# Two attention stretches per block of a squared-ReLU layer: from steps 1 and 8 to steps 3 and 10

## The chip, the cores and the metric

The kernel runs on one core of a Trainium2 chip. The metric is the device time of one execution in microseconds (us); the median of several runs is compared. TensorE (PE) does the matmuls, VectorE (DVE) and ScalarE (ACT) the element-wise work, GpSimd (POOL) gathers and scatters, and SyncE (SP) issues nearly all DMA transfers in one queue.

## The reference, cut to what matters

Three layers follow each other on 3072 tokens (4 sequences of 768) of width 384 (8 heads of 48).

```python
# 1. attention with a decaying state
state = alpha[:, :, t, :, None] * state + k_t v_t^T      # for each t
y[:, :, t] = q_t @ state
# 2. squared ReLU, 384 -> 2048 -> 384
h = x @ w_in; g = max(h, 0) ** 2; x = g @ w_out
# 3. eight experts, each token goes to one: 384 -> 1024 -> 384
e = argmax(x @ w_gate + modality_bias[modality_id])
out[e] = gate_w * (max(x[e] @ w1[e], 0) @ w2[e])
```

## The kernel before, in words

Attention is cut into 24 units `u` of 128 tokens, all heads of one sequence at a time; two sequences take turns, six units each. For one unit DVE first scans the decays (`a_scan`, `a_scan2`, lines 314 to 333: two scans, two products that scale k and q in place). Then PE does a stretch of small matmuls: `finish(u - 1)` (line 832) computes the output `py` of the unit before (lines 389 and 392) and its state update `kv` (line 374), and `a_p(u)` and `a_kt(u)` compute the scores `pp` (line 342) and a transpose `pk` (line 356). `group(u)` (line 838) is this whole stretch. ACT copies `py` to `y` (line 394), which SP writes to a DRAM scratch `yt_d` (line 397); `finish` also issues the loads of unit `u + 1`.

The squared-ReLU layer works in 12 blocks `n` of 256 tokens (two units). A block has 16 steps, one for each 128 of the 2048 inner columns. At a step PE does layer 1 (`layer1`, nine matmuls of 256 columns into `ph`, three for each of three 128-row parts, since every fp32 factor is split in a high and a low part), and then layer 2 of the step three before (`moe1_l2`, line 864, six matmuls of 392 columns into the two accumulators `po`). ACT and DVE make `g` out of `ph` (lines 985 and 992) and split it (`gh` line 996, `gl` line 998). `ph` has two buffers. `po` is two banks, and there are only two banks for it, so the first layer-2 matmul of a block (at its step 3, three steps after its first layer-1 matmul) can start only when the result of the block before has been read out of both: `lg` (line 873, DVE), then `ob` (line 874 on ACT, line 875 on DVE). That block's last layer-2 matmul is at step 2 of the present block. The input of a block comes from `yt_d`: `a_yload` (line 401, tile `xf`) reads it, and `a_x` splits it into `xh` (line 407, ACT) and `xl` (line 408, DVE), at the latest for the block's step 0.

Blocks 0 and 1 are interleaved with LEAD = 8 in the first 32 steps; the diff doesn't touch their list but for the scans of unit 7. From block 2 on every block has the two stretches of `GA` (line 772), of units 2n+3 and 2n+4, and the scans of a unit stand 4 and 2 steps ahead of its stretch. Blocks 2 to 10 hold units 7 to 23 and the last `finish`; block 11 has none. Steps are collected with `put` (line 886) and run ahead of the layer-1 matmuls of their step. Other entries of the list are the routing to experts (`ROUTE`, line 770, at steps 3, 5 and 9 to 14: `lg` to one-hot, then on PE `pr` at step 9 and `ptab` at step 13, in the PSUM bank "ms" that `kv` and `pk` also use) and the check of the decays (line 424).

The order by hand is that of PE alone: `with tc.manual_schedule(engines={mybir.EngineType.PE})` (line 974). ACT, DVE, POOL and SP get an order when the program is built, in which the place in the list is only one thing that counts, and readiness another; on the chip each then works its own queue in that order.

Of the kernel before, what the change touches and what calls it, by code (L numbers as in the profile page):

```python
# [179 lines left out]
def gla_moe_moe2(ctx: ExitStack, tc: tile.TileContext, ain, vin, al_d, wio_d, wg_d, wgt_d, mid_d, mb_d, w12_d, out):  # L180
# [133 lines left out]
    def a_scan(u):  # L314
        al, qk, v = attn_in.pop(u)
        q, k = qk[:, 0:HP * C], qk[:, HP * C:]
        ar3 = p2.tile([HR, HP, C + 1], F32, name="ar")
        ar = ar3.rearrange("p g t -> p (g t)")
        mul = dve if u < MULD else pool
        dve.tensor_tensor_scan(out=ar, data0=al[:, 0:HP * (C + 1)], data1=delta.rearrange("p g t -> p (g t)"), initial=0.0, op0=ALU.mult, op1=ALU.add)  # L320
        mul.tensor_tensor(out=k.rearrange("p (g t) -> p g t", g=HP), in0=k.rearrange("p (g t) -> p g t", g=HP), in1=ar3[:, :, 0:C], op=ALU.mult)
        ac = ar3[:, :, C:C + 1]

        inv = d1[:, 1:].rearrange("p (g t) -> p g t", g=HP)[:, :, C:]
        dve.tensor_scalar(out=inv, in0=ac, scalar1=PROD_MIN, scalar2=None, op0=ALU.max)
        dve.reciprocal(out=inv, in_=inv)
        un[u] = dict(q=q, k=k, v=v, ac=ac, al=al, mul=mul)

    def a_scan2(u):
        q, al, mul = (un[u][i] for i in ("q", "al", "mul"))  # L330
        af = p1.tile([HR, HP * (C + 1) + 1], F32, name="af")
        dve.tensor_tensor_scan(out=af, data0=al[:, ::-1], data1=d1[:, ::-1], initial=0.0, op0=ALU.mult, op1=ALU.add)
        mul.tensor_tensor(out=q.rearrange("p (g t) -> p g t", g=HP), in0=q.rearrange("p (g t) -> p g t", g=HP), in1=af[:, 1:].rearrange("p (g t) -> p g t", g=HP)[:, :, 0:C], op=ALU.mult)
# [3 lines left out]
    def a_p(u):  # L337
        x = un[u]
        pp = [ps1.tile([128, HP, C], F32, tag=t, name="pp") if u in ATG else ps2.tile([128, HP, C], F32, tag="out" if u == 1 else "P", name="pp") for t in ("ms", "y")]
        for hp in range(HP):  # L340
            for j, (r0, r1) in enumerate(((0, 64), (64, HR))):
                pe.matmul(out=pp[j][:, hp, :], lhsT=x["k"][r0:r1, hp * C:(hp + 1) * C], rhs=x["q"][r0:r1, (HP - 1 - hp) * C:(HP - hp) * C], start=True, stop=True)
        x["pt"] = []
        for j in range(2):
            if u in (1, 3):
                pt = p3.tile([128, 2, XW], F32, tag="ob", name="pt").rearrange("p j d -> p (j d)")[:, 0:HP * C].rearrange("p (g t) -> p g t", g=HP)
            else:
                pt = p1.tile([128, HP, C], F32, tag=f"pt{j}", name="pt")
            dve.tensor_tensor(out=pt.bitcast(I32), in0=pp[j].bitcast(I32), in1=mask[:, None, :].to_broadcast([128, HP, C]), op=ALU.bitwise_and)
            x["pt"].append(pt)  # L350

    def a_kt(u):
        x = un[u]
        pk = ps1.tile([128, HP, HR], F32, tag="ms", name="pk")
        for hp in range(HP):
            pe.transpose(out=pk[:, hp, :], in_=x["k"][:, hp * C:(hp + 1) * C], identity=ident[0:HR, 0:HR])
        kt = p1.tile([128, HP, HR], F32, name="kt")
        act.copy(out=kt, in_=pk)
        x["kt"] = kt

    def a_scale(u):
        if u // 2 % CPB:
            t = st_t[u % 2][:, :, 0:D]
            dve.tensor_tensor(out=t, in0=t, in1=un[u]["ac"].to_broadcast([HR, HP, D]), op=ALU.mult)
# [34 lines left out]
    def a_yload(n):  # L399
        x = p1.tile([128, ND, TB], F32, name="xf")  # L400
        sp.dma_start(out=x, in_=yt_d.rearrange("(d p) t -> p d t", p=128)[:, :, n * TB:(n + 1) * TB])
        xt[n] = x

    def a_x(n):
        xh = p2.tile([128, ND, TB], F32R, name="xh")
        xl = p2.tile([128, ND, TB], F32R, name="xl")
        act.copy(out=xh, in_=xt[n])  # L407
        dve.tensor_tensor(out=xl, in0=xt[n], in1=xh, op=ALU.subtract)  # L408
        xt[n] = (xh, xl)
# [359 lines left out]
    ROUTE0 = 14, 15, 16, 17, 18, 19, 20, 21  # L769
    ROUTE = 3, 5, 9, 10, 11, 12, 13, 14  # L770
    ROUTEZ = 3, 3, 4, 5, 6, 6, 7, 8
    GA = 1, 8
    PRE = 4
    LEAD = 8
    LAG1 = 3
# [7 lines left out]
    if True:  # L783
# [48 lines left out]
        def finish(u, load=True):  # L832
            a_y(u)
            a_state(u)
            if load and u + 2 < NU:
                load_attn(u + 2)

        def group(u):

            finish(u - 1)  # L840
            if u < NU:
                a_p(u)
                a_kt(u)
                a_scale(u)
# [41 lines left out]
        def put(gs, *steps):  # L886
            at.setdefault(gs, []).extend(steps)
# [44 lines left out]
        for n in range(2, NB):  # L932
            g0 = two + (n - 2) * NF
            for i in range(2):
                u = 2 * n + 3 + i
                if u <= NU:
                    put(g0 + GA[i] + 2 * (u == 7), lambda u=u: group(u))
                    if u < NU:
                        put(g0 + GA[i] - 4, lambda u=u: a_scan(u))
                        put(g0 + GA[i] - 2, lambda u=u: a_scan2(u))  # L940
            if n < NB - 1:
                put(g0 + 12, lambda n=n: a_yload(n + 1))
                put(g0 + 15, lambda n=n: a_x(n + 1))
        g0 = two + (NB - 3) * NF
# [10 lines left out]
        for m in range(NB - 1):  # L955
# [7 lines left out]
            g0 = two + (m - 1) * NF  # L963
            spread([g0 + k for k in (ROUTE if 0 < m < NB - 2 else ROUTE0 if m == 0 else ROUTEZ)], route())
        for i in range(NA):
            g0 = two + (3 + i // 2) * NF + 8 * (i % 2)
# [157 lines left out]
```

## Time and profile before

| | |
|---|---|
| median of 3 runs | 825.29 us (824.69 to 828.78) |
| profiled execution | 822.23 us, its span 820.4 us |
| PE, PE weight loads | busy 769.2 us (94%), 738.6 us (90%) |
| DVE, ACT, POOL | busy 543.6 us (66%), 402.6 us (49%), 64.5 us (8%) |
| DMA | 105.39 MB, mean 128 GB/s |
| mean granted TensorE clock | 0.974 |

The page gives busy time of each engine, then the span in 40 slices of 20.5 us with the busy share in tenths. Blocks 2 to 10 lie at about 148 to 538 us. Times in the rows are counted from the start of the span. A wait is the time an engine stood idle ahead of an instruction, with the instruction that released it.

### The profile page before, as it was taken

Reading aid. Unit: us, or ns where it says so; the run is one execution under the profiler, and the core shown is the slowest. Engines: PE = TensorE matmul, PEld = TensorE weight load, DVE = VectorE, ACT = ScalarE, POOL = GpSimd, SP = SyncE. Lnnn points to the kernel's source line nnn. Section 1 sums busy time; section 2 is a strip of 40 time slices with the busy share of each in tenths; the row PEclk is TensorE's granted clock in tenths of the full one; section 3 lists DMA queues with packets and bytes.
Section 4 is the critical chain, followed back from the end, with each engine's and each line's share of the span. In section 5 each row is a group of like instructions: output and inputs, shape, how many; then the busy total and the mean of one; then the engine's idle time right before and its main releaser. Section 6 shows DMA issues by size and latency. Waiting matters only on the chain. (4 is left out here: it accounts for less than half of the span.)

```text
span 820.4 us, 16492 instructions
## 1 busy us (share of the span) xinstructions
PE 769.2 (94%) x6174; PEld 738.6 (90%) x6174; DVE 543.6 (66%) x1370; ACT 402.6 (49%) x895; POOL 64.5 (8%) x85
## 2 busy tenths in 40 slices
PE   6589999999999999999999999999899999999992
PEld 4478989999998998999999999999889999999992
DVE  8889985776665664676767554456896666666631
ACT  2467879533333333333333333334666666666631
POOL 1000000000000000000000000002013322223110
PEclk9599999999999999999999999999999999999996
DMA  8877566232313211222222211105878777777600
GB/s 241 232 198 219 173 182 192 63 87 56 90 50 103 62 58 39 81 61 76 63 64 64 64 30 30 30 20 172 248 241 240 237 218 230 227 224 231 194 30 18
DMA packets 56019, 105.39 MB, mean 128 GB/s; under 512 B 9163, under 2 KB 29141, under 8 KB 55920
## 3 DMA queue, kind: packets, MB, share of 16 engines
q1 hardware_dynamic: 52720, 94.49, 39.2%
q0 software_dynamic: 3200, 9.65, 3.4%
q8 instruction: 53, 0.87, 0.5%
q14 instruction: 46, 0.38, 0.2%
HBM read 89.95 MB, written 14.36 MB: 127 GB/s over the span
## 5 line engine op out<-in xcount | busy, mean ns | idle before, releaser
L430 PE MATMUL ph<-xh,wh 128*128 128x256 f32 x864 | 249.7, 289 | 7.9 <-ACT xh L407 4.8
L430 PE MATMUL ph<-xl,wh 128*128 128x256 f32 x864 | 243.0, 281 | 1.5 <-DVE xl L408 1.5
L430 PE MATMUL ph<-xh,wl 128*128 128x256 f32 x864 | 243.0, 281 | 0.0
L430 PE MATMUL po<-wh,gh 128*128 128x392 f32 (+1 forms) x584 | 201.6, 345 | 9.4 <-ACT ob L874 5.7
L430 PE MATMUL po<-wh,gl 128*128 128x392 f32 (+1 forms) x584 | 198.3, 340 | 0.0
L430 PE MATMUL po<-wl,gh 128*128 128x392 f32 (+1 forms) x584 | 198.2, 339 | 0.0
L430 PEld LDWEIGHTS ph<-xh,wh 128*128 128x128 f32 x864 | 163.5, 189 | 10.9 <-ACT xh L407 5.1
L430 PEld LDWEIGHTS ph<-xl,wh 128*128 128x128 f32 x864 | 163.8, 190 | 1.8 <-DVE xl L408 1.8
L430 PEld LDWEIGHTS ph<-xh,wl 128*128 128x128 f32 x864 | 163.5, 189 | 0.0
L260 DVE TENSOR_TENSOR wl<-st,wh 128x768 fp32r<-128x768 f32 x104 | 99.5, 957 | 62.5 <-ACT wh L259 62.5
L996 ACT CAST gh<-g 128x256 fp32r<-128x256 f32 x192 | 77.9, 406 | 116.5 <-DVE g L992 116.1
L998 DVE TENSOR_TENSOR gl<-g,gh 128x256 fp32r<-128x256 f32 x192 | 80.8, 421 | 62.3 <-ACT gh L996 61.9
L430 PEld LDWEIGHTS po<-wh,gh 128*128 128x128 f32 x584 | 110.1, 189 | 11.5 <-ACT ob L874 6.9
L985 ACT ACTIVATE g<-ph 128x256 f32<-128x256 f32 x192 | 73.6, 383 | 94.9 <-PE ph L430 94.6
L259 ACT CAST wh<-st 128x768 fp32r<-128x768 f32 x104 | 86.7, 834 | 56.0 <-PE po L430 42.6
L992 DVE SCALAR_TENSOR_TENSOR g<-ph,g 128x256 f32<-128x256 f32 x160 | 67.3, 421 | 66.1 <-ACT g L985 65.7
L430 PEld LDWEIGHTS po<-wl,gh 128*128 128x128 f32 x584 | 110.3, 189 | 0.0
L430 PEld LDWEIGHTS po<-wh,gl 128*128 128x128 f32 x584 | 110.0, 188 | 0.2 <-DVE gl L998 0.2
L727 ACT ACTIVATE gh<-ph 128x256 fp32r<-128x256 f32 x96 | 37.0, 386 | 22.3 <-PE ph L430 20.3
L729 DVE SCALAR_TENSOR_TENSOR gl<-ph,gh 128x256 fp32r<-128x256 f32 x96 | 40.0, 417 | 8.6 <-ACT gh L727 8.5
L563 POOL IOTA row<- 1x96 f32 x1 | 0.2, 234 | 473.7 <-PE py L389 473.7
L745 POOL DMA_INDIRECT out_dram<-xs,ix x25 | 27.3, 1093 | 114.9 <-ACT xs L744 59.6
(187 smaller groups left out, 817.0 us busy)
## 6 DMA issues: line engine op xcount, KB each, us to landing
st<-in_w_dram SPq DMA_DIRECT2D x104, 384.0 KB, 3.9
st<-in_wio_dram SPq DMA_DIRECT2D x32, 384.0 KB, 4.0
qk<-in_ain_dram SPq DMA_DIRECT2D x23, 448.0 KB, 4.2
al<-in_ain_dram SPq DMA_DIRECT2D x24, 226.2 KB, 2.9
v<-in_vin_dram SPq DMA_DIRECT2D x24, 224.0 KB, 3.3
scr<-ob SPq DMA_DIRECT2D x12, 385.0 KB, 3.0
yt_d<-y SPq DMA_DIRECT2D x48, 96.0 KB, 2.8
xf<-yt_d SPq DMA_DIRECT2D x12, 384.0 KB, 3.5
```

Of the source, the lines that this page charges most:

```text
L259: act.copy(out=hi[:, 0:2 * DM], in_=t)
L260: lo_eng.tensor_tensor(out=lo[:, 0:2 * DM], in0=t, in1=hi[:, 0:2 * DM], op=ALU.subtract)
L430: pe.matmul(out=out_, lhsT=lhs[a][lsl], rhs=rhs[b][rsl], start=first and i == 0, stop=last and i == 2)
L563: pool.iota(thr, pattern=[[0, E], [SLOT, NJ]], base=0, channel_multiplier=0, allow_small_or_imprecise_dtypes=True)
L727: act.activation(out=gh[:, cols], in_=h, func=AF.Relu)
L729: dve.scalar_tensor_tensor(out=gl[:, cols], in0=h, scalar=0.0, in1=gh[:, cols], op0=ALU.max, op1=ALU.subtract)
L745: pool.indirect_dma_start(out=out[:, :], out_offset=bass.IndirectOffsetOnAxis(ap=x["ix"][:, 2 + j:3 + j], axis=0), in_=xo[:, 0:DM], in_off ...
L985: act.activation(out=g, in_=ph, func=AF.Relu)
L992: dve.scalar_tensor_tensor(out=g, in0=ph, scalar=0.0, in1=g, op0=ALU.max, op1=ALU.mult)
L996: act.copy(out=gh, in_=g)
L998: (pool if n in POOLGL else dve).tensor_tensor(out=gl, in0=g, in1=gh, op=ALU.subtract)
```

## The change

The two numbers of `GA` become 3 and 10, and the special case that put unit 7 two steps later falls away (unit 7 stands at step 3 either way). So eight stretches (units 9, 11, ... 23) move from step 1 to step 3 of blocks 3 to 10, nine (8, 10, ... 22 and the last `finish`) from step 8 to step 10 of blocks 2 to 10, and the scans of units 7 to 23 move by two steps in the list.

```diff
-    GA = 1, 8
+    GA = 3, 10
...
                 if u <= NU:
-                    put(g0 + GA[i] + 2 * (u == 7), lambda u=u: group(u))
+                    put(g0 + GA[i], lambda u=u: group(u))
                     if u < NU:
                         put(g0 + GA[i] - 4, lambda u=u: a_scan(u))
                         put(g0 + GA[i] - 2, lambda u=u: a_scan2(u))
```

## Rows read from the trace of the kernel before

**Rows 1.** The page: busy time of the engines, and the granted TensorE clock.

```profile
PE 769.2 (94%) x6174; PEld 738.6 (90%) x6174; DVE 543.6 (66%) x1370; ACT 402.6 (49%) x895; POOL 64.5 (8%) x85
...
PEclk9599999999999999999999999999999999999996
```

**Rows 2.** Waits of PE in blocks 2 to 10: us, times, longest.

```profile
PE po L430 <- ACT ob L874: 5.7, 6, 1.2
PE ph L430 <- DVE g L992: 2.2, 2, 1.9
```

**Rows 3.** Windows: step 3 of blocks 3 and 4, and the sum for blocks 3 to 8.

```profile
core 0: us, PE busy (x) PEld busy (x) DVE busy (x) ACT busy (x) POOL busy (x), PEclk, DMA share, GB/s
201.52:204.81 3.29, 2.40 (x16) 2.19 (x16) 3.22 (x15) 1.51 (x5) 0.00 (x0) 1.00 0.27 70
245.21:248.84 3.63, 2.41 (x17) 2.20 (x17) 3.63 (x17) 1.53 (x5) 0.00 (x0) 1.00 0.26 64
...
sum 20.12, PE 14.41 PEld 13.20 DVE 19.84 ACT 8.97 POOL 0.00; mean PE 2.40 PEld 2.20 DVE 3.31 ACT 1.50 POOL 0.00
```

**Rows 4.** Windows: step 3 of blocks 2, 9; block 8's steps 0 (with stretch), 4; block 5's 11.

```profile
158.48:160.90 2.42, 2.42 (x20) 2.42 (x19) 2.38 (x5) 0.92 (x2) 0.00 (x0) 1.00 0.88 249
465.19:467.49 2.30, 2.30 (x16) 2.19 (x16) 2.19 (x12) 1.36 (x5) 0.00 (x0) 1.00 0.00 0
410.79:416.95 6.16, 6.16 (x85) 5.56 (x84) 2.59 (x7) 1.78 (x4) 0.00 (x0) 1.00 0.26 75
424.60:426.73 2.13, 2.13 (x16) 2.13 (x16) 1.27 (x8) 0.56 (x2) 0.00 (x0) 1.00 0.39 144
309.94:314.17 4.23, 2.31 (x16) 1.98 (x15) 2.12 (x5) 1.21 (x4) 0.00 (x0) 1.00 0.03 9
```

**Rows 5.** Timeline, DVE, ACT and PE in steps 2 and 3 of block 8.

```profile
420.67 1.24 DVE L332 TENSOR_TENSOR_SCAN af<-al,d 112x517 f32<-112x517 f32 x1
...
422.48 0.23 DVE L873 TENSOR_TENSOR lg<-po,bias 128x8 f32<-128x8 f32 x2
...
422.90 0.47 ACT L874 COPY ob<-po 128x384 f32<-128x384 f32 x1
...
423.43 0.45 PE L430 MATMUL po<-wh,gh 128*128 128x392 f32 x1 [0.89 <-ACT ob L874]
```

**Rows 6.** Timeline, PE, DVE and ACT around the stretch of step 3 of block 2.

```profile
154.53 1.08 PE L389 MATMUL py<-qk,state 64*64 64x128 f32 x16
...
159.64 0.34 PE L430 MATMUL po<-wh,gh 128*128 128x392 f32 x1
...
154.38 0.42 DVE L873 TENSOR_TENSOR lg<-po,bias 128x8 f32<-128x8 f32 x2
...
154.81 0.47 ACT L874 COPY ob<-po 128x384 f32<-128x384 f32 x1
```

**Rows 7.** Timeline, DVE after the stretch at step 8 of block 8.

```profile
435.80 0.35 DVE L377 TENSOR_TENSOR state<-state,kv 112x192 f32<-112x192 f32 x1 [1.76 <-PE kv L374]
...
445.21 0.95 DVE L408 TENSOR_TENSOR xl<-xf,xh 128x768 fp32r<-128x768 f32 x1
...
447.30 0.43 DVE L998 TENSOR_TENSOR gl<-g,gh 128x256 fp32r<-128x256 f32 x1 [0.47 <-ACT gh L996]
```

**Rows 8.** Timeline, PE: first layer-1 matmul of block 9.

```profile
454.68 0.28 PE L430 MATMUL ph<-xh,wh 128*128 128x256 f32 x1
```

**Rows 9.** Timeline, DVE and PE: `xl` of block 5, and its first layer-1 matmul.

```profile
270.89 0.95 DVE L408 TENSOR_TENSOR xl<-xf,xh 128x768 fp32r<-128x768 f32 x1
...
278.99 0.28 PE L430 MATMUL ph<-xh,wh 128*128 128x256 f32 x1
```

**Rows 10.** Timeline, SP and ACT: the read of `xf` for block 6, and what waits.

```profile
306.77 0.33 SPq L230 DMA_DIRECT2D al<-in_ain_dram  x1
307.20 0.38 SPq L401 DMA_DIRECT2D xf<-yt_d  x1
...
311.96 0.83 ACT L407 CAST xh<-xf 128x768 fp32r<-128x768 f32 x1 [1.94 <-DMA xf<-yt_d]
312.70 0.38 ACT L985 ACTIVATE g<-ph 128x256 f32<-128x256 f32 x1
```

**Rows 11.** Waits of all engines over the span: ACT's for `xf`.

```profile
ACT xh L407 <- DMA xf<-yt_d: 5.7, 4, 2.1
```

**Rows 12.** Timeline, ACT: one of the decay checks of line 424.

```profile
109.93 0.93 ACT L424 ACTIVATE x<-st,abias 128x768 bf16<-128x768 f32 x1
```

## The prediction

> **What bounds the kernel now.** I read the page first: PE is busy 94% of the span and its weight loads 90%, DVE 66%, ACT 49% [rows 1]. So only what makes PE wait is worth anything, and the total of its matmuls doesn't change here. Next the waits of PE in the stretch that the change touches, blocks 2 to 10. There are only two kinds [rows 2]: six waits of a layer-2 matmul for the copy of `ob`, 5.7 us together, and two waits of a layer-1 matmul for a late `g`, 2.2 us. Then the windows, step by step. A plain step takes 2.13 us [rows 4]. Step 3 of blocks 3 to 8 takes 3.29 to 3.63 us, 20.12 us for the six [rows 3]; in block 9 it takes 2.30 us [rows 4]. Last the timeline of one of them [rows 5]: a scan of 1.24 us starts on DVE at 420.67, so `lg` starts only at 422.48, ACT's `ob` runs from 422.90 to 423.37, and PE, whose layer 1 of that step is done, starts `po` at 423.43. All of this is the exchange of the two `po` banks: the old result has to be out of both before the new block's first layer-2 matmul, and between the two stands one layer 1 of about 1.05 us (nine matmuls, step 3 up to 422.4). The granted clock is 1.00 in every window [rows 3, 4], so no term of mine comes from the clock.
>
> **The change, part by part.**
>
> *The stretch from step 1 to step 3, eight times.* A step with a stretch takes 6.16 us against 2.13 [rows 4], so a stretch costs PE 4.03 us wherever it stands. At step 3 it lies between the last layer-2 matmul of the old block (step 2) and the first of the new (step 3): the read-out of `po` gets 4.03 + 1.05 = 5.1 us in place of 1.05. What it needs now is 1.05 + about 1.1 = 2.2 us, so it is covered with almost 3 us to spare. Block 2 shows this arrangement already, since its stretch stands at step 3 [rows 6]: `lg` starts at 154.38, `ob` on ACT ends at 155.28, the stretch starts at 154.53, and the new `po` starts only at 159.64. Block 2 is not full proof, as its accumulators don't share the banks of the block before; but the read-out is done 4.4 us ahead of where it would be waited for. Gain: 20.12 - 6 x 2.13 = 7.3 us in blocks 3 to 8, and 2.30 - 2.13 = 0.2 us in block 9: 7.5 us.
>
> What the profile calls idle is less, 5.7 us [rows 2]. The page's own legend says that ends of matmuls are modelled; the window has no such end in it, and the first `po` matmul is drawn as 0.45 us long [rows 5]. The Trainium skill (Perfetto Trace Analysis, section Tensor Engine Instruction (MATMUL, LD_WEIGHTS)) says that a matmul's end is computed from its size and not observed. By that rule the start-to-start windows count, and the trace agrees; by the idle alone the gain would be 5.7 us, which I keep as the lower bound.
>
> *The stretch from step 8 to step 10, nine times.* Nothing waits around step 8 or 10. The distances between stretches stay: 7 steps and 9 steps, before and after. So `pt`, `kt`, the state, the loads of the next units and the slots they wait for keep their places against each other, and the `y` writes and loads on SP keep their order. SP is moved past one thing, the write of `ob` by the routing, one DMA per block, which nothing in the block waits for. POOL is passed by none of it (0.00, x0, in these windows [rows 3, 4]).
>
> What shrinks is the distance to the block's end, by two steps, 4.26 us: `y` is written, read back as `xf` and split into `xh` and `xl` for the next block's step 0. In block 8 `xl` ends at 446.16 [rows 7] and block 9 starts at 454.68 [rows 8], 8.5 us later; the tightest is block 5, with 271.84 against 278.99 [rows 9], 7.15 us. After the change 4.3 and 2.9 us are left. I cost this at nothing; what hides it is layers 1 and 2 of the last steps, and if that cover went, every us of lateness would be paid once per block, nine times.
>
> The other neighbour is the routing's `pr` at step 9, whose bank `kv` needs at step 10. DVE is the one to free it, by one small add. Ahead of `kv` PE has a step and the `py` matmuls, over 4 us, and at step 9 DVE no longer has the load that follows a stretch. Cost nothing; bound, one scan ahead of the add, 1.24 us [rows 5], of which 4 us of cover take all.
>
> *DVE after a stretch.* After the stretch at step 8 DVE is busy without a break from 435.80 until its next wait before 447.30 [rows 7], while PE in block 8 loses nothing there. At step 3 the read-out of `ob` and the small operations of the routing come on top, but they start when the stretch does, at a time when PE produces no `ph`. In block 2, with just these neighbours, step 3 takes 2.42 us [rows 4] from its layer 1 to the next, with more matmuls in it (x20) than a plain step (x16): the end of the stretch, and a `ptab`, which stands at step 4 there. So I cost it at nothing.
>
> *Unit 7's scans* stand two steps later in the list, though its stretch doesn't move. DVE's order isn't that of the list: the decay checks of the list's block 5 and later run at 109.93 [rows 12]. The bound is one scan, 1.24 us [rows 5], either way.
>
> *Sum.* 7.5 us, less 0.5 us that I take off for small new waits on a reordered DVE queue (an estimate: less than half of that one scan). The profiled execution of 822.2 us becomes 815.2 us. The median of the runs stands 3.1 us above it, at 825.3 us; the gain is the same, so 818.3 us.
>
> **The rivals.**
>
> *More late g's, small.* The late `g` is real: block 5's step 11 takes 4.23 us instead of 2.13 [rows 4]. The way it comes about [rows 10]: SP issues `al` at 306.77, when the scan that still read its slot has ended, and behind it, at 307.20, the read of `xf`. ACT's queue has `xh` next and waits 1.94 us for `xf`; the `g` behind it starts at 312.70, and PE has both `ph` buffers full. If the new order does this in two more blocks, 2 x 2.1 = 4.2 us of the 7.0 go: 822.5 us, no difference that can be told. For it: ACT waited for `xf` four times [rows 11]. Against it: only two of these reached PE [rows 2], and the change moves the whole chain as one.
>
> *The same, in every block: slower.* One mechanism, the read of `xf` behind another DMA in SP's queue, with `xh` at the head of ACT's. The break-even is 7.0 / 2.1 = 3.3 further blocks; from six on it is slower by over 0.5%. If the seven of nine blocks that don't show it now pay 2.1 us each, that is 14.7 - 7.0 = 7.7 us more than before: 833 us. The Trainium skill (Perfetto Trace Analysis, the same section) says that ACT and DVE work strictly in the order of their queues, so a waiting `xh` holds up a `g` that is ready; the trace agrees, by those 1.94 us. Against it: the waits of ACT for `xf` are 5.7 us over the whole span [rows 11], and the loads keep their distance from the stretch.
>
> *The exchange of `po` isn't relieved.* If the new queues put `lg` or ACT's `ob` behind the stretch's own work (`y`, `state`, the masks), the wait stays: 825.3 us. For it: the order of ACT and DVE is made anew when the program is built. Against it: `py`'s copy can't be ready before some 2 us of the stretch, and block 2 has `ob` first [rows 6].
>
> **How the numbers follow.** A measurement of this kernel can tell about 0.5%, 4.1 us, from no change. The forecast gets 0.76: six waits of one kind, with their length, and a cover more than twice as long. The small rival gets 0.12, the unrelieved exchange 0.05; together 0.17 within 0.5%. The slow one gets 0.07. The forecast's own range is 9.9 us of gain (7.5, and the late `g`'s in blocks 5 and 4 gone too, 2.1 and some 0.3) to 5.7 us: 815.4 to 819.6. To hold 8 in 10 I take in the small rival with 1.5 us for the spread of the medians: 815.4 to 824.0.
>
> **What would show it.** Right: no wait of `po` for `ob` in blocks 3 to 8, except perhaps in block 11; step 3 with its stretch 6.2 us up to its layer 1 and 2.2 us after; steps 1 and 8 plain. The time from a block's start to the next 43.9 us before in block 8, 42.7 us after. `xl` ends 3 to 4 us ahead of its block. Wrong: the same number of waits of `po`, a wait of a layer-1 matmul for `xh` or `xl` at a block's step 0, or late `g`'s at steps 12 to 14 in more than three blocks.

## The result, and the profile after

The changed kernel takes 814.59 us (median of 6 runs, 813.84 to 815.88), the kernel before 824.99 us beside it (6 runs): a ratio of 0.9869, 95% interval 0.9844 to 0.9894 (8.7 to 12.9 us). It is faster, as forecast, but by more than forecast: 814.59 us lies 0.8 us below the lower end of the range. The profiled execution takes 814.26 us, its span 812.5 us.

The page of the kernel after, the lines that answer to [rows 1]: PE does the same work in a shorter span, and one more slice with a lower granted clock (8 tenths) appears late in it.

```profile
PE 768.0 (95%) x6174; PEld 738.4 (91%) x6174; DVE 548.7 (68%) x1370; ACT 403.2 (50%) x895; POOL 68.0 (8%) x85
...
PEclk9599999999999999999999999999899999999997
```

The waits of PE in blocks 2 to 10 of the kernel after, beside [rows 2] (us, times, longest): the six waits of `po` for `ob` are gone, and the two late `g`'s (a layer-1 matmul that waits for a `g` to free its `ph` buffer) are down from 2.2 us to 0.9. Nothing else makes PE wait there.

```profile
PE ph L430 <- DVE g L992: 0.9, 2, 0.5
```

The window of step 3 of block 3 of the kernel after, and the sum for blocks 3 to 8, beside [rows 3] (its columns): 13.36 us in place of 20.12. Step 3 is now the step after a stretch, and takes 2.22 to 2.23 us where a plain one takes 2.13 [rows 4].

```profile
201.45:203.67 2.22, 2.22 (x18) 2.22 (x17) 2.19 (x5) 0.92 (x2) 0.00 (x0) 1.00 0.84 264
...
sum 13.36, PE 13.36 PEld 13.36 DVE 12.84 ACT 5.51 POOL 0.00; mean PE 2.23 PEld 2.23 DVE 2.14 ACT 0.92 POOL 0.00
```

Where the time went, by windows of whole blocks. First the kernel before: block 5, block 8, blocks 2 to 10 together, and all that comes behind them.

```profile
278.99:323.03 44.04, 41.22 (x350) 39.66 (x349) 28.08 (x79) 15.72 (x39) 0.00 (x0) 1.00 0.21 59
410.79:454.68 43.89, 43.00 (x381) 41.43 (x381) 28.75 (x81) 15.69 (x39) 0.00 (x0) 1.00 0.20 60
...
147.93:537.95 390.02, 382.14 (x3309) 367.53 (x3309) 246.12 (x708) 143.42 (x356) 0.52 (x2) 1.00 0.22 62
537.95:820.40 282.45, 262.62 (x1857) 259.06 (x1856) 175.45 (x394) 160.85 (x303) 61.07 (x63) 0.97 0.60 184
```

Then the same four of the kernel after.

```profile
276.24:317.61 41.37, 40.91 (x350) 39.55 (x349) 27.71 (x79) 15.62 (x39) 0.00 (x0) 1.00 0.23 63
403.25:445.96 42.71, 42.71 (x381) 41.34 (x381) 29.60 (x81) 15.73 (x39) 0.00 (x0) 1.00 0.22 61
...
147.96:529.01 381.05, 380.11 (x3309) 366.84 (x3309) 250.97 (x708) 143.86 (x356) 0.62 (x2) 1.00 0.23 63
529.01:812.50 283.49, 263.78 (x1857) 260.44 (x1856) 175.62 (x394) 160.86 (x303) 64.45 (x63) 0.97 0.61 183
```

Blocks 2 to 10 are 8.97 us shorter. A block whose only difference is the exchange of `po`, block 8, gives 1.18 us; block 5 gives 2.67 us, 1.49 us more, because its late `g` of step 11 [rows 4] is gone (a smaller one stands at step 13 now). Behind block 10 the kernel after is 1.04 us longer in this profile; the granted clock there differs from profile to profile (last section).

### The profile page after: what moved, and what is told of

Its sections match the earlier page's. It is cut to its first block, busy times and chain, and to the rows that moved or that the text cites. A ratio compares the mean times of both kernels' runs of the same rounds, so it can differ in the third digit from the quotient of the medians.

```text
span 812.5 us, 16487 instructions
## 1 busy us (share of the span) xinstructions
PE 768.0 (95%) x6174; PEld 738.4 (91%) x6174; DVE 548.7 (68%) x1370; ACT 403.2 (50%) x895; POOL 68.0 (8%) x85
## 5 line engine op out<-in xcount | busy, mean ns | idle before, releaser
L683 POOL DMA_INDIRECT xs<-scr,ix x25 | 32.5, 1301 | 69.7 <-PE px L414 24.6
```

The costliest lines, as they stand in the source:

```text
L683: pool.indirect_dma_start(out=xs[:, j, 0:XW], out_offset=None, in_=scr[0:rows, :], in_offset=bass.IndirectOffsetOnAxis(ap=ix[:, j:j + 1], ...
```

## The experiments

### Which of the two stretches

The first stretch alone is moved:

```diff
-    GA = 1, 8
+    GA = 3, 8
-                    put(g0 + GA[i] + 2 * (u == 7), lambda u=u: group(u))
+                    put(g0 + GA[i], lambda u=u: group(u))
```

> Stretches at 3 and 8: the first one is moved, the second stays. Cover (the stretch stands between the last layer-2 matmul of the old block and the first of the new): the six waits of po for ob are gone, 7.3 us of step time in blocks 3 to 8, so 6.5 to 8 us faster than before. Backlog (DVE no longer has the work after a stretch in front of lg): the same. If the second stretch carries part of the gain: the late g of block 5 (2.1 us) and block 4 (0.4 us) stays here, and this kernel lies about 1.5 us above the changed one.

Or the second alone:

```diff
-    GA = 1, 8
+    GA = 1, 10
```

> Stretches at 1 and 10: only the second one is moved. Cover and backlog: six waits of po for ob stay, 5.7 us of idle, step 3 of blocks 3 to 8 stays at 3.3 us; the time is that of before less at most 1.5 us for a shorter late g. If the second stretch carries the gain: 4 us or more faster than before.

The first alone gives 815.24 us (ratio 0.9884, 0.9855 to 0.9913), the second alone 821.38 us (0.9974, 0.9952 to 0.9995). So the first stretch carries nearly all of it. With the second alone the waits of PE in blocks 2 to 10 are those of before. The late `g`'s take 1.7 us in place of 2.2, but two further profiles of the kernel before have 1.7 and 1.8 us of them too:

```profile
PE po L430 <- ACT ob L874: 5.5, 6, 1.1
PE ph L430 <- DVE g L992: 1.7, 2, 0.9
```

### Is it the cover? Both stretches one step further

The prediction's reason was that a stretch between the old block's last layer 2 and the new block's first covers the read-out of `po`. At steps 4 and 11 the stretch runs ahead of step 4's layer 1, so it stands behind the exchange of step 3 and covers nothing of it:

```diff
-    GA = 1, 8
+    GA = 4, 11
-                    put(g0 + GA[i] + 2 * (u == 7), lambda u=u: group(u))
+                    put(g0 + GA[i] - (u == 7), lambda u=u: group(u))
```

> Stretches at 4 and 11 (unit 7 stays at 3): as late as the change and one step more, but the exchange of the po banks has no stretch in it any more. Cover: the wait of po is back, step 3 of blocks 3 to 8 about 3.3 us, and of the gain at most 1.5 us are left. Backlog: DVE has nothing but g and gl ahead of lg at step 3, as in blocks 9 and 10 of the kernel before, so step 3 takes 2.15 to 2.3 us and 6 us or more of the gain stay, without any cover.

815.72 us (0.9904, 0.9871 to 0.9937), 7.5 us below the kernel before: most of the gain is there without the cover. Its windows of blocks 2 to 10, and of one step that holds the exchange and then the stretch (block 8):

```profile
150.42:532.31 381.89, 380.53 (x3309) 366.99 (x3309) 249.90 (x708) 142.77 (x356) 0.52 (x2) 1.00 0.22 63
...
412.81:418.99 6.18, 6.18 (x84) 5.58 (x84) 4.32 (x21) 2.27 (x6) 0.00 (x0) 1.00 0.40 129
```

PE never stands still in that step. Its timeline (DVE, PE, ACT) shows what the read-out takes when nothing is in its way: the last old `po` matmul starts at 412.64, `lg` at 412.75, `ob` ends at 413.66, and the new `po` starts at 413.89 without a wait.

```profile
412.64 0.34 PE L430 MATMUL po<-wh,gl 128*128 128x392 f32 x1
...
413.89 0.34 PE L430 MATMUL po<-wh,gh 128*128 128x392 f32 x1
...
412.75 0.43 DVE L873 TENSOR_TENSOR lg<-po,bias 128x8 f32<-128x8 f32 x2
...
413.19 0.47 ACT L874 COPY ob<-po 128x384 f32<-128x384 f32 x1
```

So the question becomes what delays `lg` in the kernel before. Its timeline of DVE behind the stretch of step 1 of block 8, around the scan of [rows 5]:

```profile
415.61 0.35 DVE L377 TENSOR_TENSOR state<-state,kv 112x192 f32<-112x192 f32 x1 [1.76 <-PE kv L374]
...
418.93 0.68 DVE L321 TENSOR_TENSOR qk<-qk,ar 112x512 f32<-112x512 f32 x1
...
421.83 0.40 DVE L998 TENSOR_TENSOR gl<-g,gh 128x256 fp32r<-128x256 f32 x1
```

From 415.61 on DVE has no idle time. It is still at work on what a stretch leaves behind (state, two scans, the masks, two products: the tail of the stretch), and on the `gl` and `g` that queue up behind it, when `lg` becomes ready, some two steps later. In the kernel after the same tail comes behind the read-out (timeline of DVE, block 8):

```profile
409.58 0.42 DVE L873 TENSOR_TENSOR lg<-po,bias 128x8 f32<-128x8 f32 x2
...
412.33 0.35 DVE L377 TENSOR_TENSOR state<-state,kv 112x192 f32<-112x192 f32 x1
...
417.40 1.24 DVE L332 TENSOR_TENSOR_SCAN af<-al,d 112x517 f32<-112x517 f32 x1
```

### Bringing the delay back, first try

To steps 4 and 11, and to the change, four additions on DVE are added at step 2, which write a tile that nothing reads:

```diff
                     act.activation(out=g, in_=ph, func=AF.Relu)
+                    if n >= 3 and f == 2:
+                        dum = p1.tile([128, TB], F32, tag="wt", name="dum")
+                        for _ in range(4):
+                            dve.tensor_tensor(out=dum, in0=g, in1=g, op=ALU.add)
```

On steps 4 and 11:

> Stretches at 4 and 11 as in the run before, and four more additions of 0.42 us on DVE at step 2 of blocks 3 to 11, of which two stand ahead of the second lg and three ahead of DVE's ob; they write a tile that nothing reads. Backlog: the read-out of po, done 1.02 us after the last old matmul and needed after 1.26 us, is late by 0.6 to 1.1 us, so the wait of po for ob is back nine times and the time 5 to 10 us above the same kernel without the additions (815.7 us). If the wait needs the stretch at step 1 itself (its matmuls, its banks): no wait, time within 1.5 us.

On the change:

> The changed kernel (stretches at 3 and 10) with the same four additions on DVE at step 2 of blocks 3 to 11. Cover: the read-out is late by the same 0.6 to 1.1 us, but 5.4 us pass before the new po starts in blocks 3 to 10, so only block 11, which has no stretch, waits: the time is that of the change plus 0.5 to 1.5 us. If the stretch covers nothing: 5 us or more above the change.

819.45 us (0.9948, 0.993 to 0.9965) and 816.38 us (0.9911, 0.9892 to 0.993). The first looks like support for the theory and is none: no `po` waits in its blocks 3 to 10. Its timeline of DVE in block 8 tells why: one addition ended ahead of the first `lg` and the others fell between and behind the two, so the first `lg` started at its old distance, 0.11 us behind the start of the last old `po` matmul (412.68).

```profile
412.45 0.42 DVE L989 TENSOR_TENSOR dum<-g 128x256 f32<-128x256 f32 x1 [0.81 <-ACT g L985]
412.79 0.16 DVE L873 TENSOR_TENSOR lg<-po,bias 128x8 f32<-128x8 f32 x1
412.91 0.42 DVE L989 TENSOR_TENSOR dum<-g 128x256 f32<-128x256 f32 x1
413.25 0.15 DVE L873 TENSOR_TENSOR lg<-po,bias 128x8 f32<-128x8 f32 x1
...
543.20 0.17 PE L489 MATMUL pr<-oh,tri 128*128 128x16 bf16 x1 [1.82 <-DVE oh L473]
```

Blocks 2 to 10 take 381.45 us, no more than without the additions (381.89). The loss lies behind them, most of it at one place in block 11, the last row, in both kernels: there the routing follows the read-out at once, and `pr` waited 1.8 us for a DVE that was late, 0.2 us without the additions. The granted clock behind that wait was 0.58 for 4.07 us (0.60 for 4 us on the change), where it is 1.00 at steps 4 and 11 without them. An addition that the order is free to place tests nothing; the next pair forces it.

### Bringing the delay back, forced

`lg` now reads a copy of the bias that a fifth operation makes from the last addition's tile, so it can't start before them. The same edit on steps 4 and 11 (no cover) and on the change (cover):

```diff
+        late = {}
...
+                    if n >= 3 and f == 2:
+                        dum = p1.tile([128, ND * 128], F32, tag="wt", name="dum")
+                        for _ in range(4):
+                            dve.tensor_tensor(out=dum[:, 0:TB], in0=g, in1=g, op=ALU.add)
+                        late[n - 1] = dum[:, TB:TB + 2 * E].rearrange("p (j e) -> p j e", j=2)
+                        dve.scalar_tensor_tensor(out=late[n - 1], in0=dum[:, 0:2 * E].rearrange("p (j e) -> p j e", j=2), scalar=0.0, in1=bias[:, 2 * n - 2:2 * n, :], op0=ALU.mult, op1=ALU.add)
...
-                    dve.tensor_tensor(out=lg[:, j, :], in0=po[j][:, DM:], in1=bias[:, 2 * n + j, :], op=ALU.add)
+                    dve.tensor_tensor(out=lg[:, j, :], in0=po[j][:, DM:], in1=late[n][:, j, :] if n in late else bias[:, 2 * n + j, :], op=ALU.add)
```

Without the cover:

> Stretches at steps 4 and 11, and in blocks 3 to 11 four additions of 128x256 on DVE and one small operation whose result lg reads in place of the bias, so that lg can't start before them (the four write a tile that nothing else reads; the outputs are the reference's). They start when ACT has made the g of step 2, about 0.3 us before lg does without them, and take 4 x 0.34 + 0.1 = 1.4 us, so lg comes about 1.1 to 1.2 us late, as it does in the kernel before behind the scan of 1.24 us. Theory (the wait of po is a read-out that DVE starts late, whatever makes it late): PE waits for ob at step 3 of blocks 3 to 10, 0.9 to 1.1 us each in start-to-start time, 7 to 9 us in blocks 3 to 10, and block 11 loses another 3 to 5 us as it did with the free additions: 825 to 830 us beside 815.7 for the kernel without the additions. Rival (the exchange has slack enough that a read-out 1.2 us late is absorbed, and the gain of the change came from somewhere else): no wait of po, blocks 2 to 10 as long as without the additions, and only block 11 longer: about 819.5 us, as with the free additions.

With it:

> The change (steps 3 and 10) with the same five operations ahead of lg in blocks 3 to 11. Theory (a stretch in the exchange also covers a late read-out): ob is then done some 3 us ahead of the first po of the new block, so PE waits for it nowhere in blocks 3 to 10, which stay within 1.5 us of the change's 381; block 11, whose exchange has no stretch in it, loses 3 to 5 us: 817 to 820 us, at least 6 us less than the same additions without the cover. Rival (late DVE work costs PE by another way, through g and the ph buffers or the routing): waits of layer 1 for g, or of pr for oh, in blocks 3 to 10 as well, and a time of over 822 us, near that of the run without the cover.

832.43 us (1.0122, 1.009 to 1.0154) and 817.04 us (0.9925, 0.9898 to 0.9952). Without the cover, the waits of PE for `ob` in blocks 2 to 10, the windows of blocks 2 to 10 and of step 3 of block 8, and the timeline of that step (DVE, ACT, PE):

```profile
PE po L430 <- ACT ob L875: 11.0, 7, 1.6
PE po L430 <- DVE ob L876: 1.6, 1, 1.6
```

```profile
147.83:544.47 396.64, 382.57 (x3310) 367.60 (x3309) 262.90 (x748) 142.83 (x356) 0.52 (x2) 1.00 0.21 61
...
419.47:427.49 8.02, 6.44 (x84) 5.64 (x84) 5.96 (x26) 2.27 (x6) 0.00 (x0) 1.00 0.19 59
```

```profile
419.06 1.80 DVE L990 TENSOR_TENSOR dum<-g 128x256 f32<-128x256 f32 x4 [0.81 <-ACT g L986]
...
421.33 0.23 DVE L874 TENSOR_TENSOR lg<-po,dum 128x8 f32<-128x8 f32 x2
...
421.76 0.47 ACT L875 COPY ob<-po 128x384 f32<-128x384 f32 x1
...
422.28 0.45 PE L430 MATMUL po<-wh,gh 128*128 128x392 f32 x1 [1.58 <-ACT ob L875]
```

The wait is back in every block from 3 to 10, and the step is 8.02 us long in place of 6.18: 1.84 us, eight times, is 14.7 us, and blocks 2 to 10 grew from 381.89 to 396.64 us, 14.75. It is twice the 7 to 9 us expected: the delay was costed at 1.1 to 1.2 us, but the additions took 1.80 us, and the `g` of step 2, which stands behind them, also ran ahead of `lg`. So `lg` started 2.04 us after the start of the last old matmul (419.29), in place of 0.11.

With the cover, the waits of PE over the same stretch of the kernel show the `po` wait once only, in block 11 (none up to 538 us), and the window of block 8 from step 2's layer 1 to step 3's, with the stretch in it, is 6.18 us, against 6.17 in the change without the additions. Blocks 2 to 10 take 382.14 us, 1.1 more than in the change:

```profile
PE po L430 <- ACT ob L875: 1.6, 1, 1.6
PE ph L430 <- DVE g L999: 1.5, 2, 1.0
```

```profile
408.40:414.58 6.18, 6.18 (x85) 5.58 (x84) 4.76 (x17) 2.28 (x6) 0.00 (x0) 1.00 0.26 76
```

So both hold: a read-out that DVE starts late is what makes PE wait, and a stretch in the exchange covers it. In the changed kernel there is little left to cover, since the move also took DVE's tail out of the way.

### The slower issue of `xf`

The rival that went to the other side was a read of `xf` that comes late to `xh` at the head of ACT's queue. On the change, its DMA is issued by GpSimd:

```diff
-        sp.dma_start(out=x, in_=yt_d...)
+        pool.dma_start(out=x, in_=yt_d...)
```

> The changed kernel with the read of xf issued by GpSimd and not by SyncE, so that it stands behind no al load and no qk load. If the order of SP's queue makes xf late: in the read for block 6 the 1.9 us between the landing of y and the issue of xf go, ACT no longer waits for xf there, and the late g of block 5 (0.5 us of PE) with it; up to 1.2 us faster than the change in all. If the reads are late for another reason (their own 3.3 us, a load at the same time, the slower issue by GpSimd), ACT still waits and the time is that of the change or up to 1 us more.

823.81 us (1.0007, 0.9988 to 1.0026; 12 runs, 816.95 to 826.55): the whole gain is gone in the median. In its profile the chain is later: `xf` lands 4.0 us after its issue (median), 3.3 us in the changed kernel. ACT's waits for it in blocks 2 to 10 rise to 10.1 us from 5.1, and PE's for a late `g` to 2.4 us from 0.9 (waits of ACT and of PE; the page's DMA issues):

```profile
ACT xh L407 <- DMA xf<-yt_d: 10.1, 7, 2.8
...
PE ph L430 <- DVE g L992: 2.4, 3, 1.4
...
xf<-yt_d POOLq DMA_DIRECT2D x12, 384.0 KB, 4.0
```

The profiled execution is the fastest of the twelve (816.95 us), and shows 1.5 us of late `g` more. What the other eleven lost on top, up to 9.6 us, no profile shows. Their mean granted clock is lower (0.965 to 0.971, against 0.973 to 0.977 for the change), which fits late `g`'s that are followed by a lower clock; that is argued, not shown.

### Taking `xh` and `xl` out of the way

On the change, for blocks 3 and later:

```diff
-        act.copy(out=xh, in_=xt[n])
-        dve.tensor_tensor(out=xl, in0=xt[n], in1=xh, op=ALU.subtract)
+        if n < 3:
+            act.copy(out=xh, in_=xt[n])
+            dve.tensor_tensor(out=xl, in0=xt[n], in1=xh, op=ALU.subtract)
+        else:
+            pool.tensor_copy(out=xh, in_=xt[n])
+            pool.tensor_tensor(out=xl, in0=xt[n], in1=xh, op=ALU.subtract)
```

> The changed kernel with both operations of a_x (xh and xl) on GpSimd from block 3 on, so that no xh stands in ACT's queue and no xl in DVE's. If a waiting xh in ACT's queue makes the late g: no wait of a layer-1 matmul for g is left in blocks 2 to 10 (0.9 to 1.1 us of idle in the two profiles of the change), and the time is 0.5 to 1.5 us below the change. If GpSimd needs more than the 4.7 us that xl is early, the block's first matmuls wait for it, up to several us per block: slower than the change. If DVE and GpSimd slow each other: DVE's operations beside it take longer than 0.42 us.

812.66 us (0.9861, 0.983 to 0.9892; 6 runs, 811.53 to 813.44), below all other kernels here and some 2 us under the change, whose interval overlaps (0.9844 to 0.9894). The reason given for it did not hold: with `xh` out of ACT's queue the late `g`'s are still there, two waits of 1.1 us together, and blocks 2 to 10 take as long as in the change (windows of blocks 2 to 10 and of what follows).

```profile
148.18:529.20 381.02, 379.92 (x3309) 366.94 (x3309) 250.02 (x699) 137.35 (x347) 25.99 (x20) 1.00 0.23 63
529.20:809.80 280.60, 261.28 (x1857) 257.64 (x1856) 175.28 (x394) 160.50 (x303) 62.16 (x63) 0.98 0.61 185
```

Its profile is 2.89 us shorter than the change's behind block 10 (280.60 against 283.49), where a lower clock is missing this time. Whether the split itself is worth anything is open.

### The two kernels again

The unchanged kernel was run as an experiment of its own, the change again (on another chip than the first experiments), and the kernel before was profiled twice more.

> The kernel before, unchanged, for the spread of its runs: median within 1.5 us of the other median, single runs 822 to 829 us. If the 2.4 us by which the medians differ more than the two profiles (10.4 against 8.0) come from reads of xf that are late by chance, this profile shows other late g's than those of blocks 4 and 5, of up to 2 us each; if not, its blocks 2 to 10 take 390.0 us again and the difference lies ahead of them or behind.

> The changed kernel, unchanged, beside the kernel before on one chip. If the forecast missed because it stood on a median of three runs (825.3 us) that lies above that of many runs (823.2 us for 23), the medians here differ by 8 to 9 us: 1.5 us of it from shorter waits for a late g, 7.3 us from step 3. If the gain really is 10.4 us as in the first comparison, they differ by 10 us or more.

> The kernel before once more, for its profile alone. The timed gain (about 10 us) is 1 to 2 us above that of the profiled blocks 2 to 10 (8.9 us). If late g's of about 2 us in block 5 let the clock fall, as in the run with stretches at 3 and 8, this profile can show a granted clock of 0.5 after such a wait, 1.7 us in a step of blocks 4 to 6; if not, blocks 2 to 10 take 389.5 to 390.0 us as in the other two profiles.

> The kernel before, a fourth profile. As in the run ahead of it: either a granted clock of 0.5 somewhere in blocks 4 to 6 behind a late g, at 1.7 us, or 389.5 to 390.0 us for blocks 2 to 10.

Before against itself: 824.04 us, ratio 0.9999 (0.9979 to 1.0018). The change: 814.13 us, 0.9879 (0.9863 to 0.9896). The two further profiles of the kernel before took 820.94 and 822.69 us, their blocks 2 to 10 389.35 and 389.50 us at a granted clock of 1.00: no wait for a late `g` was followed by a lower clock there. Windows of blocks 2 to 10 and of what follows, in the second profile of before and the second of the change:

```profile
147.59:537.11 389.52, 381.69 (x3309) 367.42 (x3309) 246.41 (x708) 143.30 (x356) 0.52 (x2) 1.00 0.21 62
537.11:818.10 280.99, 260.94 (x1857) 257.63 (x1856) 175.31 (x394) 160.88 (x303) 56.78 (x63) 0.98 0.57 185
```

```profile
148.15:529.27 381.12, 380.00 (x3309) 366.84 (x3309) 250.68 (x708) 143.92 (x356) 0.62 (x2) 1.00 0.23 63
529.27:812.70 283.43, 264.03 (x1857) 260.28 (x1856) 175.49 (x394) 160.80 (x303) 61.38 (x63) 0.97 0.61 183
```

Blocks 2 to 10 repeat to 0.7 us (389.35 to 390.02 in four profiles before; 381.05 and 381.12 after). The medians of before, over the 6, 23, 17, 11 and 7 runs beside the other kernels, are 824.99, 823.21, 823.0, 823.48 and 823.13 us; over all 64 runs 823.2 us. The 11 runs of the change have the median 814.45 us. The gain is thus 8.8 us, inside the interval of the first comparison, and blocks 2 to 10 are 8.2 to 9.0 us shorter.

## Why the prediction came out as it did

**The step that failed.** It is the sum, in two of its terms: the anchor, a median of three runs (825.3 us, where 64 runs give 823.2), and the 0.5 us taken off for new waits, where the late `g`'s got shorter instead (7.0 us of gain forecast, 8.8 measured). Both are taken up below. Half of the reason given for the main term failed too; its size came out right all the same, since either reason brings step 3 back to a plain step.

**The bound.** Right: PE's work didn't change, the waits did, and they were the two kinds named.

**The exchange of `po`, 7.5 us.** Right in size: 1.18 us per block in block 8, where nothing else differs, against the 3.29 - 2.13 = 1.16 us of one step [rows 3, 4]; six such steps fell from 20.12 to 13.36 us. Block 8 takes 42.71 us, forecast 42.7. That windows from start to start count, and not the 5.7 us drawn as idle, was right too.

**Its reason, the cover.** Half of it fails. "What it needs now is 1.05 + about 1.1 = 2.2 us" took a queue for a duration. In the kernel before `lg` starts 1.36 us after the last old matmul (421.12), and `po` 2.31 us after it; some 1.1 us of this are `lg` waiting behind DVE's tail of the stretch two steps earlier. Undisturbed, `lg` starts 0.11 us after, and `po` 1.25 us after (412.64 to 413.89 at steps 4 and 11), without any wait. Moving the tail off the read-out is enough: step 4, which covers nothing, gives most of the gain. The cover itself is real; the forced pair shows it.

Why ACT's `ob` waits for DVE's `lg`, though both only read `po`, the trace shows but does not explain: in the free additions `ob` starts 0.03 us after the end of the first `lg` (412.95), with ACT idle for 0.56 us before, and the profile names `lg` as what released it. The Trainium skill (PSUM — Partial Sum Buffer, section PSUM bank collisions raise a hardware error) says that no two engines may access one PSUM bank on the same partitions at the same time, reads included, and that a scheduler therefore puts their accesses in order. The traces agree: in the rows shown here ACT's `ob` never starts before the `lg` of its bank has ended.

**The stretch from step 8 to 10, at nothing.** Near enough: alone it is worth 1.8 us at the median (0.4 to 4.0). Its blocks 2 to 10 take 388.73 us, 0.6 to 1.3 less than the four profiles of the kernel before, and its waits for a late `g` are as long as in two of these; where the rest lies is open.

**The margin of `xl`.** Forecast to shrink to 4.3 us, 2.9 at the tightest; it shrank less, to between 4.4 and 6.3 (the sign named was 3 to 4). For block 9 `xl` ends at 440.61, and the block starts at 445.96. Nothing waited, as forecast.

**Unit 7's scans, at nothing.** Right: block 2 takes 43.06 us, before 43.08. The row given for the order of DVE [rows 12] is one of ACT, so it shows that ACT's order isn't that of the list, and not DVE's.

**DVE at nothing.** Right in blocks 2 to 10. What a late DVE costs where there is no cover, the forced pair shows: 1.6 us of wait per block.

**"7.5 us, less 0.5 us that I take off for small new waits".** Here a term failed. No new kind of wait came, and the late `g`'s got shorter: block 5 gives 1.49 us beyond the exchange between the first two profiles, 0.7 between the closest two (43.75 and 41.86 us). That gain stood in the range, "2.1 and some 0.3", but not in the forecast. Forecast 7.0 us, measured 8.8. Why the late `g`'s got shorter is open; the split of `xh` and `xl` speaks against the reason that was tried.

**"The median of the runs stands 3.1 us above it, at 825.3 us".** This is the larger failure, 2.1 us: three runs gave 825.3, 64 give 823.2. Of the first six runs five lie at 824.6 us or above, of the 70 of the later comparisons 17; whether that was bad luck or something about that first occasion, the runs don't tell. The working allowed 1.5 us for the spread of medians at the upper end only. 823.2 less the 9.9 us of the forecast's own lower bound is 813.3 us, and 814.59 lies above that.

**The rivals.** More late `g`'s: not more, but shorter ones. The slow chain of `xf` in every block did not come; that a later `xf` has a price here, 1.5 us of late `g`, the issue by GpSimd shows. The unrelieved exchange did not come; it is what the second stretch alone looks like.

## What to carry to other kernels

When PE waits for a read-out, take apart how much of the wait is the read-out's own work and how much is another job's tail on the engine that does it: the first asks for cover, the second only for another place of that job. Anchor a forecast on many runs, or on the profiled stretch that the change touches, and carry the spread of the anchor to both ends of the range. An experiment that adds load has to force its place by a dependence, and the trace has to show where it stood before its time is read.

## What the runs showed of the hardware that was not expected

**A wait may or may not be followed by a lower granted clock.** At the end of the squared-ReLU layer, about 579 us in the kernel before and 571 us after, PE waits for the last `gh`. Windows that begin where that wait ends: the kernel before (2.71 us of wait), its second profile (1.75 us), the change (2.64 us; its second profile has 2.47 us and the same clock).

```profile
579.80:583.00 3.20, 3.10 (x12) 3.10 (x13) 2.16 (x4) 1.45 (x4) 0.00 (x0) 0.53 0.71 200
```

```profile
579.20:583.00 3.80, 3.71 (x27) 3.71 (x28) 3.62 (x10) 2.98 (x7) 0.00 (x0) 1.00 0.71 217
```

```profile
570.70:577.50 6.80, 6.62 (x28) 6.62 (x29) 4.44 (x11) 3.65 (x9) 0.00 (x0) 0.53 0.65 200
```

The granted clock (the third number from the end) is near the lower level, 1.2 GHz, for 3.2 us, not at all, and for 6.8 us. With `xh` on GpSimd the wait is 2.54 us and the clock stays at the upper level, 2.4 GHz: 50 matmuls run in 570.7 to 577.5, 28 in the change. The missing 22 are worth 3.0 us by an estimate (6.80 us / 50 each), which is about what the two profiles differ by behind block 10, 2.89 us. The 1 us between the change and the first profile of before is no cost of the change: another profile of before takes 283.45 us there.

**The same in the dense blocks.** With the first stretch alone, the late `g` of block 5 (1.96 us) is followed by a step at a low clock, 4.00 us in place of the 2.43 of the same step in the kernel before (314.17 to 316.60); there the same wait, 1.9 us [rows 2, 4], is not followed by one. Nor are the eight waits of 1.6 us of the forced pair without the cover (granted clock 1.00), while the 1.8 us in block 11 with the free additions are (0.58).

```profile
304.96:309.22 4.26, 2.39 (x17) 2.06 (x15) 2.17 (x5) 1.27 (x3) 0.00 (x0) 1.00 0.04 10
309.22:313.22 4.00, 3.92 (x17) 3.92 (x18) 2.06 (x6) 1.88 (x5) 0.00 (x0) 0.57 0.01 2
```

**GpSimd's price for the split.** In its kernel the copy `xh` takes 0.91 us on average and the subtraction `xl` 1.91 us, against 0.83 us on ACT and 0.96 us on DVE in the change (groups of blocks 2 to 10, POOL; the page calls spans on POOL rough):

```profile
L412 POOL TENSOR_TENSOR xl<-xf,xh 128x768 fp32r<-128x768 f32 x9 | 17.2, 1914 | 0.7
L411 POOL CAST xh<-xf 128x768 fp32r<-128x768 f32 x9 | 8.1, 905 | 463.6 <-DMA xf<-yt_d 283.8 <-DVE gl L1002 179.9
```

The Trainium skill (GPSIMD Engine Reference, section 4.1 Engine selection) says that an element-wise operation with two inputs is about twice as slow on GpSimd as on VectorE. The trace agrees: 1.91 against 0.96 us. For one with a single input the same section of the Trainium skill says that GpSimd runs at roughly line rate; no run here has the copy `xh` on VectorE to compare with.
